# Weight loads on the hardware queue and a rearranged prologue, in a Fourier transform with a maxout layer

## The chip, the cores and the metric

The kernel runs on one core of a Trainium2 chip. The metric is the device time of one execution in microseconds (us), as the median of several runs. Engine names are those of the profile: PE multiplies matrices, DVE is the vector engine, ACT the scalar engine, POOL is GpSimd, SP starts transfers. POOL starts transfers too, on the software queue (q0 in the profile). SP's transfers go through the hardware queue (q1).

## The reference

```python
x: (8, 3072, 256) float32
X = fft(x, axis=1);  X = fft(X, axis=2);  y = X.real        # 2-D Fourier transform, real part
y = y.reshape(24576, 256)
h = maximum(maximum(y @ w1, y @ w2), y @ w3)                # w1, w2, w3: 256 x 768
out = h @ w_out                                             # w_out: 768 x 256
```

## The kernel before

Each of the 8 batches is one Fourier transform of 3072 rows. It is split as 24 × 128: stage `s` (`Mix.s`, L474 and L476) multiplies the rows of x by small 24-point tables, with the rows in forward order (`nat` for batch 0, `x0` after that) and in reversed order (`back`, the second half of `x0`). ACT or DVE evict the result to `z` (L481). Stage `k` (`Mix.k`, L500 and L502) multiplies `z` by the tables `tab`, and ACT evicts to `t` (L504). The tables have 13 rows of three parts each: a sine, a shifted sine, and the first part negated (`tab_minus`, L272).

The transform over the 256 columns is linear, so it is folded into the weights. With its table `md`, `prep_first` makes from `d2 = w2 - w1` and `d3 = w3 - w1` the folded weights `gE` (even part), `gO` (odd part) and `gD` (`gO` times a column `dif`). Half `jh` 0 or 1 of the 768 hidden columns is done at a time, four PE banks each: `gE` is evicted by DVE (L419), `gO` by ACT, and `gD` by DVE from `gO` (L422). `prep_second` folds `w1` and `w_out` together: `g1t` (L433, three evictions), then `gw` (L442, L447), then `twice` (L451).

Each batch has 18 units: 3 blocks of 512 frequencies by 6 groups `jc` of 128 hidden columns. In a unit PE makes the sums for one half of the spectrum (`unit_plus`, L520 and L521), ACT writes their ReLU to `stmp` (L534), DVE takes the maximum with the second sum (L535, to `hp`); then PE adds `gD` (`unit_minus`, L528) and ACT and DVE do the same for the mirrored half, to `hm`. The second layer is spread over later units: `l2_even` and `l2_odd` (L558, L569), `l2_hidden` (L545); DVE makes `other` (L572) and `ot` (L595), POOL makes `even` (L575) and scatters the mirrored rows with an indirect transfer (L598).

Each engine's program is in the order in which the kernel is written out (`manual_schedule`); an engine that waits holds up all that is behind it. What is done between units is set by a hand-written table, `at(batch, unit, function)`: at a unit's end the functions entered for it write their instructions.

Before the first unit there is a prologue. POOL loads x of batch 0 in 16 transfers that also convert to bfloat16, in four groups of rows (0 to 31, 32 to 63, 64 to 95, 96 to 111; rows 112 to 127 come by other queues into `xs_a`). Then it loads the weights in halves, `w1`, `w2`, `w3` of half 0 and then of half 1 (L204). DVE and ACT meanwhile compute the tables and copy x into `nat` (`lay_rows`, L345) and `back` (`turn_rows`, L133). PE multiplies tables (35 `warm` matmuls, L691) until x is laid out. SP loads the four chunks of batch 1 (`load_chunk`, L102) behind the weights of half 0 (`first_half`). POOL converts and turns chunks 0 to 2 (`turn_chunk`, L148 and L151); chunk 3 is split between ACT (L159) and POOL (L161) in `turn_last`. `differences` (L174) is done by DVE for half 0 and by POOL for half 1. `store_rows` computes the row numbers for the scattered stores (`rows_m`).

Of the kernel before, what the change touches and what calls it, by code (L numbers as in the profile page):

```python
# [9 lines left out]
FP32 = mybir.dt.float32  # L10
# [23 lines left out]
def kernel(  # L34
# [51 lines left out]
    half_pi = consts.tile([128, 64], FP32, tag="half_pi")  # L86
    w_late = consts.tile([128, 3 * 128], FP32, tag="w_late")
    twice = consts.tile([128, 256], FP32, tag="twice")
# [9 lines left out]
    def load_rows(engs, dst, b, r0, r1, after=None):  # L98
        xr = x_rows(b)
        for g in range(4):  # L100
            eng = engs[g] if isinstance(engs, tuple) else engs
            ld = eng.dma_start(out=dst[g * 24:(g + 1) * 24], in_=xr[g, :, r0:r1, :])  # L102
            if after is not None:
                tc.add_manual_dep(ld.ins, after.ins.name, AFTER, reason="weights first")

    def load_next(eng, dst, b, after=None):
# [18 lines left out]
    raw = {}  # L125
# [43 lines left out]
    def cols(t, jh):  # L169
        return t.rearrange("p (fc j) -> p fc j", fc=2)[:, :, jh * 384:(jh + 1) * 384]  # L170
# [26 lines left out]
    for r0 in (0, 32, 64):  # L197
        load_rows(nc.gpsimd, x0v[:, r0:r0 + 32, :], 0, r0, r0 + 32)
    load_rows(nc.gpsimd, x0v[:, 96:112, :], 0, 96, 112)

    first_half = None
    for jh in range(2):
        for wsrc, wdst in zip((moe_w1, moe_w2, moe_w3), (w1_bf, *raw_w)):
            wld = nc.gpsimd.dma_start(  # L204
                out=cols(wdst, jh),
                in_=wsrc.rearrange("(fc p) j -> p fc j", fc=2)[:, :, jh * 384:(jh + 1) * 384])
        if jh == 0:
            first_half = wld
    rows_f = gen.tile([128, 12 * B], FP32, tag="rows_f")
# [14 lines left out]
    for (name, value) in (("rnd", ROUND), ("n24", -24.0)):  # L224
# [18 lines left out]
                                   op0=ALU.add, op1=ALU.subtract)  # L243
    w = gen.tile([128, 10 * 128], FP32, tag="w")
    turn = 2.0 * math.pi

    def rows_of(r0, r1):
        return (w_late if r0 >= 10 else w)[:, (r0 % 10) * 128:(r0 % 10 + r1 - r0) * 128]

# [73 lines left out]
    for (m, c, own) in ((m0f, 0, 1), (m0r, 24, 3)):  # L323
        for (o0, o1, src, by) in ((0, 24, t24[:, 48 + c:72 + c], amp[:, 0:1]),
                                  (24, 26, t24[:, c:c + 13:12], amp[:, 1:2]),
                                  (26, 50, t24[:, c:c + 24], ind24[:, own:own + 1])):
            nc.scalar.activation(out=m[:, o0:o1], in_=src, func=AX.Copy, scale=by)

    tab_minus(0, 7)
    nc.vector.tensor_scalar(out=sgn, in0=pidx, scalar1=0.0, scalar2=None, op0=ALU.is_equal)  # L330
    nc.vector.tensor_scalar(out=sgn, in0=sgn, scalar1=2.0, scalar2=-1.0,
                            op0=ALU.mult, op1=ALU.add)
    nc.vector.tensor_scalar(out=dif, in0=sgn, scalar1=1.0, scalar2=None, op0=ALU.subtract)

# [9 lines left out]
    def lay_rows(copy, xs, r0, n, d0=0, d1=33):  # L344
        copy(out=xn0[:, d0:d1, r0:r0 + n],  # L345
             in_=bass.AP(xs.tensor, xs.offset + d0, [xs.ap[0], [1, d1 - d0], [64, n]]))

    def bf_rows(r0, n):
# [7 lines left out]
    tab_angles(7, 10)  # L356
    tab_angles(10, 13)
    lay_rows(on_act, bf_rows(0, 32), 0, 32)
# [3 lines left out]
    dvec = gen.tile([128, 128], FP32, tag="dvec")  # L362
    nc.vector.scalar_tensor_tensor(
        out=dvec.rearrange("p (dl g) -> p dl g", g=4),
        in0=j128[:, 0:4].unsqueeze(1).to_broadcast([128, 32, 4]), scalar=64.0,
        in1=j128[:, 0:32].unsqueeze(2).to_broadcast([128, 32, 4]), op0=ALU.mult, op1=ALU.add)
    nc.vector.tensor_scalar(out=dvec[:, 2:4], in0=j128[:, 0:2], scalar1=64.0, scalar2=32.0,
                            op0=ALU.mult, op1=ALU.add)
    vm = gen.tile([128, 256], FP32, tag="vm")
    qm = gen.tile([128, 256], FP32, tag="qm")  # L370
    nc.vector.tensor_scalar(out=vm[:, 0:128], in0=dvec, scalar1=pidx, scalar2=64.0,
                            op0=ALU.mult, op1=ALU.add)
    nc.vector.tensor_scalar(out=vm[:, 128:256], in0=dvec, scalar1=pidx, scalar2=None,
                            op0=ALU.mult)
    nc.vector.tensor_scalar(out=vm[:, 128:129], in0=pidx, scalar1=128.0, scalar2=64.0,
                            op0=ALU.mult, op1=ALU.add)
    turn_rows(on_act, 63, 32, 54, 65)
    turn_rows(on_dve, 63, 32, 32, 54)
    lay_rows(on_dve, bf_rows(64, 32), 64, 32)
    tab_sines(7, 10, (2,))  # L380
    tab_sines(10, 13, (0,))
    for (copy, a, b, c, d) in ((on_dve, 32, 54, 0, 20), (on_act, 54, 64, 20, 33)):
        turn_rows(copy, 95, 17, a, b)
        if copy is on_act:
            turn_rows(copy, 95, 16, 64, 65)
        lay_rows(copy, bf_rows(96, 16), 96, 16, c, d)
    nc.vector.tensor_scalar(out=qm, in0=vm, scalar1=256.0 * ROUND, scalar2=None, op0=ALU.add)
    nc.vector.scalar_tensor_tensor(out=vm, in0=qm, scalar=-256.0 * ROUND, in1=vm,
                                   op0=ALU.add, op1=ALU.subtract)

    for ch in range(4):
        raw[1, ch] = load_chunk(1, ch, first_half)
    tab_minus(7, 10, nc.gpsimd)
    nc.gpsimd.memset(two_row, 0.0)
# [5 lines left out]
    nc.gpsimd.dma_start(out=wout_bf.rearrange("p (jc c) -> p jc c", jc=NJC),  # L400
# [5 lines left out]
    def prep_first(jh, bank):  # L406

        cs = slice(jh * 384, (jh + 1) * 384)
        for i, wv in enumerate((d2_bf, d3_bf)):
            for half in range(2):  # L410
                psg = bank()
                hs = slice(half * 128, (half + 1) * 128)
                for fc in range(2):
                    nc.tensor.matmul(
                        psg[:, 0:384], md[fc][:, hs],
                        wv[:, fc * DFF + jh * 384: fc * DFF + jh * 384 + 384],
                        start=(fc == 0), stop=(fc == 1))
                if half == 0:
                    nc.vector.tensor_copy(out=gE[i][:, cs], in_=psg[:, 0:384])  # L419
                else:  # L420
                    nc.scalar.copy(out=gO[i][:, cs], in_=psg[:, 0:384])
                    nc.vector.tensor_scalar(out=gD[i][:, cs], in0=gO[i][:, cs], scalar1=dif,  # L422
                                            scalar2=None, op0=ALU.mult)
                yield

    def prep_second():

        for jp in range(NJC // 2):
            pst = ps_f.tile([128, 512], FP32, name="pst", tag="ps")
            for k in range(2):  # L430
                jc = jp * 2 + k
                for fc in range(2):
# [18 lines left out]
        nc.tensor.matmul(pst[:, 0:256], two_row, gw[:, 256:512], start=True, stop=True)  # L451
        nc.vector.tensor_copy(out=twice, in_=pst[:, 0:256])
        nc.vector.tensor_scalar(out=twice[:, 0:1], in0=twice[:, 0:1], scalar1=-1.0, scalar2=None,
                                op0=ALU.add)
# [234 lines left out]
    warm = ps_s.tile([128, 512], FP32, name="warm", tag="ps")  # L689
    for _ in range(35):  # L690
        nc.tensor.matmul(warm, tab[:, 0:128], tab[:, 0:512], start=True, stop=True)  # L691
    m = Mix(0)
    x0f = (lambda d: xn0[:, d, 0:128], rows_back(xr0))
    for k in range(7):
        m.s(k, x0f, pool=ps_s if k % 4 else ps_f,
            evict=nc.vector.tensor_copy if k in (1, 3) else nc.scalar.copy)
        if k == 1:
            differences(nc.vector, 0, (0,))
        if k == 2:
            nc.scalar.activation(out=md[0], in_=vm, func=AX.Sin, scale=float(-2.0 * math.pi / 256.0))  # L700
        if k == 3:
            halves = [t.rearrange("p (q two g) -> p two q g", two=2, g=4) for t in md]
            nc.vector.tensor_copy(out=halves[1][:, 0], in_=halves[0][:, 0])
            nc.vector.tensor_scalar(out=halves[1][:, 1], in0=halves[0][:, 1], scalar1=-1.0,
                                    scalar2=None, op0=ALU.mult)
            differences(nc.vector, 0, (1,))
    slots = [ps_s, ps_s, ps_f, ps_f]
# [58 lines left out]

    def late_tables():
        tab_sines(10, 13, (1, 2))
        tab_minus(10, 13, nc.gpsimd)

    for (u, fn) in ((0, prep_some), (0, prep_some), (1, prep_some), (1, prep_some),
                    (2, lambda: m.k(2)), (2, late_tables), (2, prep_some), (2, prep_some),
                    (3, lambda: m.k(3)), (3, prep_some), (4, prep_some),
                    (5, prep_some), (5, l2_first),
                    (6, lambda: m.k(4)), (7, lambda: m.k(5)), (7, m.end),
                    (0, lambda: turn_chunk(1, 0)), (2, lambda: turn_chunk(1, 1)),
                    (5, lambda: turn_chunk(1, 2)),
                    (8, lambda: turn_last(0)), (9, lambda: turn_last(1))):
        at(0, u, fn)
# [92 lines left out]
```

## Time and profile before

| what | value |
|---|---|
| median of 3 runs | 417.44 us (417.38 to 417.55) |
| the profiled execution | 417.16 us, its span 415.3 us |
| granted PE clock, mean | 0.999 |
| PE busy | 397.7 us, 96% |
| DVE, ACT, POOL busy | 313.1, 266.8, 320.4 us |
| chain that ended last | PE 88%, POOL 4%, DVE 4% |
| first real matmul (L474) | 19.29 us |
| first `gE`/`gO` matmul of a unit (L520) | 24.95 us |
| PE at stage `s0` of batch 1 | arrives 53.19 us, goes on 54.49 us |

The span runs from the first to the last instruction; 1.86 us of the profiled execution lie outside it. A timeline row has start, duration, engine, line, operation, tiles, shape and count; in brackets is the engine's idle time before it and what ended that. A row of waits reads: who waited, for what, total us, times, longest.

### The profile page before, as it was taken

The page shows a single profiled execution, that of the slowest core. Times are in us where ns is not written, and L with a number is a line of the kernel's source. Part 1 is how long each engine was busy: PE and PEld are TensorE (multiplying, and loading weights), DVE is VectorE, ACT ScalarE, POOL GpSimd, SP SyncE. Part 2 cuts the span into 40 slices and gives each one's busy share as a digit, 9 for nine tenths or more (in the row PEclk, how much of TensorE's full clock was granted, in tenths as well). Part 3 has the DMA queues.
Part 4 walks back from the last instruction along what each step waited for, and adds up shares of the span by engine and source line. Part 5 has one row for each costly group of instructions (what it writes and reads, how often), then busy time and mean ns, then how long its engine had stood idle before and what let it go on. Part 6 is the DMA issues. An engine that isn't in the chain of part 4 may idle for free.

```text
span 415.3 us, 9110 instructions
## 1 busy us (share of the span) xinstructions
PE 397.7 (96%) x3076; PEld 269.0 (65%) x3076; DVE 313.1 (75%) x561; ACT 266.8 (64%) x488; POOL 320.4 (77%) x431
## 2 busy tenths in 40 slices
PE   1889989999999999999999999999999999999996
PEld 0455667666676677667666666666676667766665
DVE  8998766776777777687668767687678777778883
ACT  7777767666766666666775666666676666655550
POOL 9977867999988888888878788888878844445651
PEclk9999999999999999999999999999999999999999
DMA  9998895684327841396316852288312222111314
GB/s 112 165 202 176 177 230 123 153 198 109 113 76 181 199 140 65 102 218 162 104 64 165 202 112 106 88 207 179 121 52 76 66 67 76 66 65 47 108 64 140
DMA packets 130535, 52.70 MB, mean 127 GB/s; under 512 B 113073, under 2 KB 127224, under 8 KB 130488
## 3 DMA queue, kind: packets, MB, share of 16 engines
q1 hardware_dynamic: 105408, 35.93, 35.7%
q0 software_dynamic: 24144, 15.86, 16.7%
q8 instruction: 24, 0.39, 0.5%
q10 hardware_dynamic: 936, 0.33, 0.3%
q14 instruction: 23, 0.19, 0.2%
HBM read 29.02 MB, written 25.17 MB: 130 GB/s over the span
## 4 chain that ended last, share of the span: by engine, by line
PE 88%; POOL 4%; DVE 4%; issue 2%; DMA 1%; ACT 1%; POOLq 0%; DVEq 0%; ACTq 0%
PE po L545 29%; PE pse L520 14%; PE pse L528 14%; PE pse L521 14%; PE ps L476 2%; PE ps L502 2%; PE ps L474 2%; PE ps L500 2%; PE po L569 2%; PE pl L558 2%; POOL x L102 2%; DMA x<-in_x_dram 1%; DVE gD L422 1%; DMA out_dram<-ot 1%; DVE back L133 1%
## 5 line engine op out<-in xcount | busy, mean ns | idle before, releaser
L534 ACT ACTIVATE stmp<-pse 128x512 bf16<-128x512 f32 x288 | 171.3, 600 | 42.5 <-PE pse L521 29.6
L535 DVE TENSOR_TENSOR hp<-pse,stmp 128x512 bf16<-128x512 f32 x144 | 99.5, 691 | 89.0 <-ACT stmp L534 60.7
L598 POOL DMA_INDIRECT out_dram<-ot,rows_m x92 | 102.6, 1115 | 53.6 <-DVE ot L595 41.6
L520 PE MATMUL pse<-t,gE 128*128 128x512 bf16 x288 | 109.2, 379 | 2.0 <-DVE hm L535 0.7
L521 PE MATMUL pse<-t,gO 128*128 128x512 bf16 x288 | 109.0, 378 | 0.0
L535 DVE TENSOR_TENSOR hm<-pse,stmp 128x512 bf16<-128x512 f32 x144 | 99.1, 688 | 3.6 <-ACT stmp L534 3.5
L575 POOL TENSOR_TENSOR even<-even,other 128x256 f32<-128x256 f32 x92 | 66.4, 722 | 26.4 <-DVE other L572 23.3
L545 PE MATMUL po<-wout_bf,hp 128*128 128x256 bf16 x576 | 85.9, 272 | 0.0
L528 PE MATMUL pse<-t,gD 128*128 128x512 bf16 x288 | 85.6, 379 | 0.0
L545 PE MATMUL po<-wout_bf,hm 128*128 128x256 bf16 x570 | 85.3, 273 | 0.0
L545 PEld LDWEIGHTS <-hp 128*128 128x128 bf16 x576 | 56.3, 98 | 17.6 <-issue 2.4
L545 PEld LDWEIGHTS <-hm 128*128 128x128 bf16 x576 | 56.4, 98 | 16.5
L595 DVE TENSOR_TENSOR ot<-po,even 128x512 f32<-128x512 f32 x92 | 62.8, 683 | 0.3 <-POOL even L575 0.3
L148 POOL CAST x<-xs 96x544 bf16<-96x544 f32 (+2 forms) x51 | 58.6, 1155 | 4.0 <-DMA xs<-in_x_dram 4.0
L151 POOL CAST x<-xs 96x544 bf16<-96x544 f32 (+5 forms) x57 | 60.5, 1071 | 0.0
L504 ACT CAST t<-ps 128x512 bf16<-128x512 f32 x48 | 28.0, 586 | 36.1 <-PE ps L502 34.8
L481 ACT CAST z_all<-ps 128x480 bf16<-128x480 f32 x46 | 25.6, 559 | 37.8 <-PE ps L476 35.7
L528 PEld LDWEIGHTS <-gD 128*128 128x128 bf16 x288 | 27.9, 98 | 32.2
L572 DVE SCALAR_TENSOR_TENSOR other<-twice,po 128x256 f32<-128x256 f32 x92 | 43.8, 476 | 0.1
L521 PEld LDWEIGHTS <-gO 128*128 128x128 bf16 x288 | 28.1, 98 | 21.2 <-issue 2.9
L520 PEld LDWEIGHTS <-gE 128*128 128x128 bf16 x288 | 28.1, 98 | 20.2 <-DVE gE L419 1.0
L561 ACT COPY even<-pl 128x512 f32<-128x512 f32 x46 | 27.0, 588 | 9.7 <-PE pl L558 9.4
(166 smaller groups left out, 390.5 us busy)
## 6 DMA issues: line engine op xcount, KB each, us to landing
xs<-in_x_dram SPq DMA_DIRECT2D x84, 198.0 KB
out_dram<-ot SPq DMA_DIRECT2D x90, 128.0 KB
xs<-in_x_dram SPq DMA_DIRECT2D x28, 192.0 KB
raw_w<-in_moe_w_dram POOLq DMA_DIRECT2D x4, 384.0 KB
out_dram<-ot,rows_m POOLq DMA_INDIRECT x92
x<-in_x_dram POOLq DMA_DIRECT2D x12, 96.0 KB
out_dram<-ot SPq DMA_DIRECT2D x17, 64.0 KB
xs<-in_x_dram SPq DMA_DIRECT2D x32, 5.8 KB
```

Source lines behind the costliest of these rows:

```text
L148: nc.gpsimd.tensor_copy(v[:, d0:d1, ch * 32:ch * 32 + 32], xs[:, 0:32 * 64].rearrange("p (bb dl) -> p dl bb", dl=64)[:, d0:d1, :])
L151: reverse(lambda out, in_: nc.gpsimd.tensor_copy(out, in_), v[:, 33:66, :], xs, ch * 32, 33 if ch == 3 else 32, 32 + d0, 32 + d1)
L520: nc.tensor.matmul(pse[:, 0:n], gE[i][:, js], te, start=True, stop=False)
L521: nc.tensor.matmul(pse[:, 0:n], gO[i][:, js], to, start=False, stop=True)
L528: nc.tensor.matmul(pse, gD[i][:, js], to, start=False, stop=True, skip_group_check=True)
L534: nc.scalar.activation(out=stmp[:, 0:n], in_=pses[0][:, 0:n], func=AX.Relu)
L535: nc.vector.tensor_tensor(out=dst, in0=src3, in1=stmp[:, 0:n], op=ALU.max)
L545: nc.tensor.matmul(po, hcols(jc), wout_bf[:, jc * 256:(jc + 1) * 256], start=False, stop=(jc == NJC - 1), skip_group_check=True)
L572: nc.vector.scalar_tensor_tensor(out=other, in0=twice, scalar=po[:, 256:257], in1=po[:, 0:256], op0=ALU.mult, op1=ALU.subtract)
L575: nc.gpsimd.tensor_tensor(out=line[:, 256:512], in0=line[:, 0:256], in1=other, op=ALU.add)
L595: nc.vector.tensor_tensor(out=ot, in0=po, in1=lin, op=ALU.add)
L598: stored(nc.gpsimd.indirect_dma_start(out, bass.IndirectOffsetOnAxis(ap=rows_m[0:128 - lo, b * 12 + slot: b * 12 + slot + 1], axis=0), ot[ ...
```

## The change

- `w1` of half 0 stays on POOL behind x. `w2` and `w3` of both halves are loaded by SP; those of half 0 wait for the third group of x. `w1` of half 1 is loaded by POOL after `store_rows`. The chunks of batch 1 follow on SP without a wait of their own.
- A memset of `mark` on POOL waits for DVE's last copy of `nat`; POOL's memsets, `store_rows`, `w1` of half 1, `differences` and `w_out` stand behind it.
- In the last copies ACT and DVE have other shares. `dvec` goes ahead of `tab_minus(0, 7)`; `vm` and `qm` go ahead of the third group's copies on DVE, `sgn` and `dif` behind the last; the sine for `md` goes ahead of the third group on ACT.
- `gD` is made from PSUM. The first `g1t` and 255 columns of `twice` are evicted by ACT.
- The third part of the tables' rows 7 to 9 and the first part of rows 10 to 12 are made in units 0 and 2, the rest of rows 10 to 12 in unit 3. POOL's `tab_minus` for them goes to units 1 and 3; `k3` goes from unit 3 to unit 4; the first of the three `g1t` steps goes from unit 2 to unit 1. `turn_last` goes from units 8 and 9 to units 7 and 8.
- There are 32 warm matmuls.

```diff
-    first_half = None
+    load_w(nc.gpsimd, w1_bf, moe_w1, 0)      # load_w: the same transfer, on a given queue
     for jh in range(2):
-        for wsrc, wdst in zip((moe_w1, moe_w2, moe_w3), (w1_bf, *raw_w)):
-            wld = nc.gpsimd.dma_start(...)
-        if jh == 0:
-            first_half = wld
+        for wsrc, wdst in zip((moe_w2, moe_w3), raw_w):
+            ld = load_w(nc.sync, wdst, wsrc, jh)
+            if jh == 0:
+                tc.add_manual_dep(ld.ins, third.ins.name, AFTER, reason="x first")
...
+    (dvec, two instructions, from below)
     tab_minus(0, 7)
-    (sgn, dif: three instructions)
...
     tab_angles(10, 13)
+    (vm[:, 0:128], from below)
     lay_rows(on_act, bf_rows(0, 32), 0, 32)
     tab_sines(7, 10, (0, 1))
     turn_rows(on_dve, 31, 32, 32, 65)
     lay_rows(on_dve, bf_rows(32, 32), 32, 32)
-    (dvec; vm[:, 0:128])
     (vm[:, 128:256]; vm[:, 128:129])
-    turn_rows(on_act, 63, 32, 54, 65)
-    turn_rows(on_dve, 63, 32, 32, 54)
-    lay_rows(on_dve, bf_rows(64, 32), 64, 32)
-    tab_sines(7, 10, (2,))
-    tab_sines(10, 13, (0,))
-    for (copy, a, b, c, d) in ((on_dve, 32, 54, 0, 20), (on_act, 54, 64, 20, 33)):
+    (qm; vm rounded, from below)
+    nc.scalar.activation(out=md[0], in_=vm, func=AX.Sin, scale=...)
+    for (copy, a, b, c, d) in ((on_act, 54, 65, 20, 33), (on_dve, 32, 54, 0, 20)):
+        turn_rows(copy, 63, 32, a, b)
+        lay_rows(copy, bf_rows(64, 32), 64, 32, c, d)
+    for (copy, a, b, c, d) in ((on_act, 58, 64, 22, 33), (on_dve, 32, 58, 0, 22)):
         turn_rows(copy, 95, 17, a, b)
         if copy is on_act:
             turn_rows(copy, 95, 16, 64, 65)
-        lay_rows(copy, bf_rows(96, 16), 96, 16, c, d)
-    (qm; vm rounded)
+        laid = lay_rows(copy, bf_rows(96, 16), 96, 16, c, d)
+    (sgn, dif)
     for ch in range(4):
-        raw[1, ch] = load_chunk(1, ch, first_half)
-    tab_minus(7, 10, nc.gpsimd)
+        raw[1, ch] = load_chunk(1, ch)
+    first_op = nc.gpsimd.memset(mark, 0.0)
+    tc.add_manual_dep(first_op.ins, laid.ins.name, AFTER, reason="the two share a port")
     (memsets of two_row, gw)
     store_rows()
+    load_w(nc.gpsimd, w1_bf, moe_w1, 1)
     differences(nc.gpsimd, 1)
...
                     nc.scalar.copy(out=gO[i][:, cs], in_=psg[:, 0:384])
-                    nc.vector.tensor_scalar(out=gD[i][:, cs], in0=gO[i][:, cs], scalar1=dif,
+                    nc.vector.tensor_scalar(out=gD[i][:, cs], in0=psg[:, 0:384], scalar1=dif,
...
-            nc.vector.tensor_copy(out=g1t[:, jp * 512:(jp + 1) * 512], in_=pst)
+            (nc.vector.tensor_copy if jp else nc.scalar.copy)(
+                out=g1t[:, jp * 512:(jp + 1) * 512], in_=pst)
...
-        nc.vector.tensor_copy(out=twice, in_=pst[:, 0:256])
-        nc.vector.tensor_scalar(out=twice[:, 0:1], in0=twice[:, 0:1], ...)
+        nc.scalar.copy(out=twice[:, 1:256], in_=pst[:, 1:256])
+        nc.vector.tensor_scalar(out=twice[:, 0:1], in0=pst[:, 0:1], ...)
...
-    for _ in range(35):                      # warm
+    for _ in range(32):
...
         if k == 1:
-            differences(nc.vector, 0, (0,))
-        if k == 2:
-            nc.scalar.activation(out=md[0], in_=vm, func=AX.Sin, scale=...)
-        if k == 3:
             (md's other half: two copies)
+            differences(nc.vector, 0, (0,))
+        if k == 3:
             differences(nc.vector, 0, (1,))
...
-    def late_tables():
-        tab_sines(10, 13, (1, 2))
-        tab_minus(10, 13, nc.gpsimd)
-    for (u, fn) in ((0, prep_some), (0, prep_some), (1, prep_some), (1, prep_some),
-                    (2, lambda: m.k(2)), (2, late_tables), (2, prep_some), (2, prep_some),
-                    (3, lambda: m.k(3)), (3, prep_some), (4, prep_some),
-                    (5, prep_some), (5, l2_first),
+    for (u, fn) in ((0, prep_some), (0, prep_some), (0, lambda: tab_sines(7, 10, (2,))),
+                    (1, prep_some), (1, prep_some), (1, prep_some),
+                    (2, lambda: m.k(2)), (2, prep_some), (2, lambda: tab_sines(10, 13, (0,))),
+                    (3, prep_some), (3, lambda: tab_sines(10, 13, (1, 2))),
+                    (4, lambda: m.k(3)), (4, prep_some), (5, prep_some), (5, l2_first),
                     (6, lambda: m.k(4)), (7, lambda: m.k(5)), (7, m.end),
-                    (0, lambda: turn_chunk(1, 0)), (2, lambda: turn_chunk(1, 1)),
+                    (0, lambda: turn_chunk(1, 0)), (1, lambda: tab_minus(7, 10, nc.gpsimd)),
+                    (2, lambda: turn_chunk(1, 1)), (3, lambda: tab_minus(10, 13, nc.gpsimd)),
                     (5, lambda: turn_chunk(1, 2)),
-                    (8, lambda: turn_last(0)), (9, lambda: turn_last(1))):
+                    (7, lambda: turn_last(0)), (8, lambda: turn_last(1))):
```

Lines in parentheses stand for instructions that are moved or kept unchanged.

More of the change, by code (lines that the diff above doesn't have):

```diff
@@ L327 @@
             nc.scalar.activation(out=m[:, o0:o1], in_=src, func=AX.Copy, scale=by)
+    dvec = gen.tile([128, 128], FP32, tag="dvec")
+    nc.vector.scalar_tensor_tensor(
+        out=dvec.rearrange("p (dl g) -> p dl g", g=4),
+        in0=j128[:, 0:4].unsqueeze(1).to_broadcast([128, 32, 4]), scalar=64.0,
+        in1=j128[:, 0:32].unsqueeze(2).to_broadcast([128, 32, 4]), op0=ALU.mult, op1=ALU.add)
+    nc.vector.tensor_scalar(out=dvec[:, 2:4], in0=j128[:, 0:2], scalar1=64.0, scalar2=32.0,
+                            op0=ALU.mult, op1=ALU.add)
     tab_minus(0, 7)
[L330 to L333, printed above, removed]
     back = gen.tile([96, 33 * 130], BF16, tag="back")
@@ L344, in lay_rows @@
     def lay_rows(copy, xs, r0, n, d0=0, d1=33):
-        copy(out=xn0[:, d0:d1, r0:r0 + n],
-             in_=bass.AP(xs.tensor, xs.offset + d0, [xs.ap[0], [1, d1 - d0], [64, n]]))
+        return copy(
+            out=xn0[:, d0:d1, r0:r0 + n],
+            in_=bass.AP(xs.tensor, xs.offset + d0, [xs.ap[0], [1, d1 - d0], [64, n]]))
     def bf_rows(r0, n):
@@ L357 @@
     tab_angles(10, 13)
+    vm = gen.tile([128, 256], FP32, tag="vm")
+    qm = gen.tile([128, 256], FP32, tag="qm")
+    nc.vector.tensor_scalar(out=vm[:, 0:128], in0=dvec, scalar1=pidx, scalar2=64.0,
+                            op0=ALU.mult, op1=ALU.add)
     lay_rows(on_act, bf_rows(0, 32), 0, 32)
@@ L361 @@
     lay_rows(on_dve, bf_rows(32, 32), 32, 32)
[L362 to L372, printed above, removed]
     nc.vector.tensor_scalar(out=vm[:, 128:256], in0=dvec, scalar1=pidx, scalar2=None,
@@ L385 @@
             turn_rows(copy, 95, 16, 64, 65)
-        lay_rows(copy, bf_rows(96, 16), 96, 16, c, d)
-    nc.vector.tensor_scalar(out=qm, in0=vm, scalar1=256.0 * ROUND, scalar2=None, op0=ALU.add)
-    nc.vector.scalar_tensor_tensor(out=vm, in0=qm, scalar=-256.0 * ROUND, in1=vm,
-                                   op0=ALU.add, op1=ALU.subtract)
+        laid = lay_rows(copy, bf_rows(96, 16), 96, 16, c, d)
+    nc.vector.tensor_scalar(out=sgn, in0=pidx, scalar1=0.0, scalar2=None, op0=ALU.is_equal)
+    nc.vector.tensor_scalar(out=sgn, in0=sgn, scalar1=2.0, scalar2=-1.0,
+                            op0=ALU.mult, op1=ALU.add)
+    nc.vector.tensor_scalar(out=dif, in0=sgn, scalar1=1.0, scalar2=None, op0=ALU.subtract)
     for ch in range(4):
-        raw[1, ch] = load_chunk(1, ch, first_half)
-    tab_minus(7, 10, nc.gpsimd)
+        raw[1, ch] = load_chunk(1, ch)
+    first_op = nc.gpsimd.memset(mark, 0.0)
+    tc.add_manual_dep(first_op.ins, laid.ins.name, AFTER, reason="the two share a port")
     nc.gpsimd.memset(two_row, 0.0)
@@ L451, in prep_second @@
         nc.tensor.matmul(pst[:, 0:256], two_row, gw[:, 256:512], start=True, stop=True)
-        nc.vector.tensor_copy(out=twice, in_=pst[:, 0:256])
-        nc.vector.tensor_scalar(out=twice[:, 0:1], in0=twice[:, 0:1], scalar1=-1.0, scalar2=None,
+        nc.scalar.copy(out=twice[:, 1:256], in_=pst[:, 1:256])
+        nc.vector.tensor_scalar(out=twice[:, 0:1], in0=pst[:, 0:1], scalar1=-1.0, scalar2=None,
                                 op0=ALU.add)
```

21 lines of the change are left out of this document (13 added, 8 removed).

## The prediction

> **What bounds the kernel now.** I read the page first: TensorE (PE) is busy for 96% of the span and carries 88% of the chain that ended last.
>
> ```profile
> PE 397.7 (96%) x3076; PEld 269.0 (65%) x3076; DVE 313.1 (75%) x561; ACT 266.8 (64%) x488; POOL 320.4 (77%) x431
> ...
> PE 88%; POOL 4%; DVE 4%; issue 2%; DMA 1%; ACT 1%; POOLq 0%; DVEq 0%; ACTq 0%
> ```
>
> Then the waits of PE. Cut to the first 56 us, the view gives all that the whole run has but 0.5 us: 0.24 at 75.09 on `t` and 0.26 at 92.15 on `ot`, both made from PE's own results shortly before, so they move along with PE.
>
> ```profile
> PE warm L691 <- DVE sgn L330: 8.9, 1, 8.9
> PE ps L474 <- DVE nat L345: 1.2, 1, 1.2
> PE ps L476 <- POOL x L161: 1.1, 1, 1.1
> PE pse L520 <- DVE hm L535: 0.7, 2, 0.4
> PE pse L520 <- DVE gE L419: 0.5, 1, 0.5
> ...
> PE psg L414 <- DVE md_all L704: 0.3, 1, 0.3
> ```
>
> So from some 55 us on PE runs practically without a wait, and no edit touches that part. The change is worth exactly the shift of PE's arrival there. I take the first matmul behind stage `s0` of batch 1 as the finish line: L520 at 54.88. The timeline of PE gives the stations before it.
>
> ```profile
> 19.29 0.20 PE L474 MATMUL ps<-m24f,nat 96*128 96x96 bf16 x1 [1.23 <-DVE nat L345]
> ...
> 26.54 0.81 PE L414 MATMUL psg<-d_bf,md_all 128*128 128x384 bf16 x4
> ...
> 53.19 0.21 PE L474 MATMUL ps<-m24f,x 96*128 96x96 bf16 x1
> 54.49 0.22 PE L476 MATMUL ps<-m24r,x 96*128 96x96 bf16 x1 [1.09 <-POOL x L161]
> ```
>
> The second station needs `d2` of weight half 1, which POOL makes from `w1` and `w2`; here PE does not wait for it. Last I read POOL's timeline, then DVE's and ACT's.
>
> ```profile
> 14.85 0.76 POOL L204 DMA_DIRECT2D w_bf<-in_moe_w_dram  x1
> ...
> 17.02 1.26 POOL L204 DMA_DIRECT2D w_bf<-in_moe_w_dram  x1
> ...
> 20.89 0.22 POOL L394 MEMSET two_row<- 128x128 bf16 x1
> ...
> 22.84 0.79 POOL L220 CAST rows_m<-rows_f 128x96 int32<-128x96 f32 x1
> 23.82 1.64 POOL L174 TENSOR_TENSOR d_bf<-raw_w,w_bf 128x768 bf16<-128x768 f32 x1 [0.19 <-DMA raw_w<-in_moe_w_dram]
> ...
> 27.42 0.93 POOL L400 DMA_DIRECT2D wout_bf<-in_moe_w_out_dram  x1
> ```
>
> ```profile
> 16.76 1.41 DVE L345 COPY nat<-x 96x1056 bf16<-96x1056 bf16 x1
> ...
> 23.43 0.54 DVE L419 CAST gE<-psg 128x384 bf16<-128x384 f32 x1
> 23.91 1.66 DVE L422 TENSOR_SCALAR gD<-gO,dif 128x384 bf16<-128x384 bf16 x1
> ...
> 28.58 0.31 DVE L422 TENSOR_SCALAR gD<-gO,dif 128x384 bf16<-128x384 bf16 x1
> ```
>
> ```profile
> 47.95 1.14 ACT L159 CAST x<-xs 96x544 bf16<-96x544 f32 x1
> ```
>
> The same `gD` costs 0.31 alone and 1.66 while POOL runs L174 (23.82 to 25.46): the two engines shut each other out when both work from SBUF.
>
> **The change, part by part.** *Start of PE's real work.* DVE's last copy of `nat` ended at 19.15. Third and fourth copies there took 0.90 + 1.41 + 0.62 + 0.51 = 3.44 us beside POOL's issues; the 1056-element copy took 1.07 at 13.57, so a quiet one saves about 0.3, and cutting columns off DVE's share (`nat` 33 to 20 columns in the third, more `back` in the fourth) saves a further 0.4 on DVE, with ACT's share fitting because two sines (0.61 and about 0.5) leave it. `dvec` and `vm` go ahead of copies that wait for data; `qm` and its partner (0.69) also move ahead, so they eat part. I put the end of DVE's copies at 18.4 (18.1 to 18.9) and PE's start at 18.45, 0.85 earlier. The three fewer warm matmuls (0.65 us) and `dvec`'s delay of the warm start by about 0.4 lie inside PE's idle 1.23: nothing; without that cover they would cost their size.
>
> *PE up to `d2` of half 1.* 26.54 less 0.85, less the stall on `md_all` (0.34; its sine now stands ahead of the third copies), less the one on `gE` (0.55; `gD` ahead of it costs 0.54, `gE`'s row from the same PSUM shape, in place of 1.66): PE could be there at 24.8. `w2` and `w3` of half 0 are read by DVE at about 20.3 and landed at 19.30 and 20.62 before, with `w1` of half 1 behind them; SP issues them from 15.3, behind the third quarter of x. The same bytes in the same order: nothing.
>
> *The new wait.* `w1` of half 1 was issued at 17.02. Now it stands on POOL behind the `mark` that waits for DVE's last copy (18.4), and behind memsets, iotas and `rows_m`: 20.89 to 23.63, 2.74 us. Queued behind it on POOL are `d2`, `d3`, `wout` and all of batch 1's turning; PE waits for `d2`. The issue costs 0.76 (bounds 0.76 and 1.26, the two rows of `w1`; I take the first, since no tail of x is issued then). From the end of the issue to landing, no row has this situation. `w1` of half 0: 15.60 to 18.35, 2.75. `wout`, twice the bytes, issued while SP's chunks were moving: 28.35 to 32.90, 4.55. Two halves of weights landed 1.0 apart, which with 0.75 of start gives 1.75 as a floor. I take 2.75, same size and queue, and keep 1.75 and 4.55. Then `d2`, 1.64, and 0.15 for hand-overs: 18.4 + 2.74 + 0.76 + 2.75 + 1.64 + 0.15 = 26.44 against 26.54. The whole lead of 1.7 is eaten: -0.1.
>
> The Trainium skill speaks here ("DMA: Bandwidth & Descriptors", Queues, rings and completion order): a DMA engine takes turns, packet by packet, between the queues that have work. By it `w1` would share with SP's chunks, its 1.2 us of transfer would double, and the sum below would end 1.2 higher, near 417.9. The trace disagrees: from 30.5 to 32.0 the software queue (`wout`) moved 150 to 167 GB/s while the hardware queue, with chunks issued, got 1 to 28.
>
> The same skill ("SBUF — State Buffer", the trap of DVE blocking DMA) says that a DVE operation holding the shared port keeps GpSimd from writing descriptors. That would make 1.26 the price of the issue, 0.5 more; the two rows of `w1` (0.76 and 1.26, the second beside DVE's copies) agree in direction.
>
> *From there to `l2`.* DVE is relieved of `gD` (four rows, 1.66 + 1.63 + 0.31 + 1.24 = 4.84, to 4 × 0.54 = 2.16), of one `g1t` (0.68) and of `twice` (0.42). Little of that is on the path: PE's stalls at 30.13 (0.41, on a `stmp`) and 32.27 (0.24, on ACT's `t`). I count 0.45 of these 0.65, since ACT takes over `g1t` (about 0.6) and `twice` (about 0.45) and two late sines: -0.45. `tab_minus` of rows 7 to 10 now stands behind the turning of chunk 0: 33.6 + 1.2 gives 34.8, and `k3`, moved from 34.00 to unit 4, comes at about 35.2. `wout` lands near 33.8; it is read from 35.7. Both margins are under 2 us and shrink with each us that `w1` is late; if POOL is a further 0.5 late, `k3` waits.
>
> *Units 7 to 9.* ACT's two copies of the last chunk (1.14 and 1.09) go one unit earlier, so the first now stands behind `t` (0.59) and `t_mid` (0.17), ahead of unit 7's two ReLUs, which before started at 46.81. They end some 1.06 later; DVE's `hp`, `hm` and the L595 that frees `po` queue behind, and PE has almost no slack there: +1.05 (bounds 0 and 1.14).
>
> *Start of batch 1.* POOL's reversals (1.16 and 1.19) follow ACT's chunk and one `even` fewer stands before the last: done by 52.9 at the latest. The wait of 1.09 goes; from L474 at 53.19 to L476 at 54.49 it is 1.30, against 0.05 unhindered: -1.25. Next to be late is nothing that I can see; PE arrives at 53.7.
>
> **Sum.** -0.1 - 0.45 + 1.05 - 1.25 = -0.75. The profiled execution took 417.16 (span 415.3, 1.86 around it), so 416.41; it was 0.28 under the median of the runs, 417.44, so 416.7 on the median's scale. 0.83 us (0.2%) is about what a measurement can tell here.
>
> **Rivals.**
> *Cheaper.* `w1` lands in 1.75 rather than 2.75 (-1.0), or ACT's copy finds slack in unit 7 (-1.05). For: halves of weights did land 1.0 apart at 300 to 400 GB/s. Against: `w1` of half 0 needed 2.75, and ACT had no gap over 0.32 between 44.0 and 51.5. Either gives 415.7.
> *Slower: `w1` behind the traffic.* SP is now free to start chunks at about 19 to 20, so the queues are full when `w1` is issued. If it needs `wout`'s 4.55, `d2` is ready at 28.24, 1.7 later than PE was there before; with -0.45 + 1.05 - 1.25 the run ends 1.05 later and `k3` waits up to 0.5 more: 418.2 to 418.8, say 418.5. It decides from the point where `w1` takes over 4.3 us (the sum passes +0.83). For: `wout`'s row is the only one beside SP's chunks. Against: it has twice the bytes, and the software queue went ahead of the other. The turn-taking rule above, with 3.95, would end below that point.
> *The silence doesn't shorten the copies.* If the hardware weight loads delay x's last rows (landed 16.78), DVE ends at 19.2 as before; `mark` and everything on POOL is 0.8 later: 417.5.
>
> **How the numbers follow.** Forecast 0.46, by itself 416.0 to 417.2, spread half and half over the bound of 416.61 (0.22 faster, 0.24 same). Cheaper 0.25, faster. Slower 0.19 (0.18 slower, 0.01 same). No shorter copies 0.10 (0.07 same, 0.03 slower). Faster 0.47, same 0.32, slower 0.21. The range reaches from below the cheaper case, 415.4, to 418.4, just short of the worst; both cheap ends at once (414.7) and the worst are left out.
>
> **What would show it.** Right: the first L474 near 18.45 without more than 1 us of idle; `gD` at 0.54 in all four rows; a new PE wait at L414 on POOL L174 of 1 to 2 us, starting near 24.8 and ending near 26.4; a wait of about 1 us near units 8 and 9 that leads back to ACT L159; no wait at L476. Wrong: PE waiting at L414 past 27.5, or at `k3` for POOL's L272 (slower); no wait at L414, or none near unit 9 (cheaper); any wait of PE after 56 us that was not there before.

## The result and the profile after

The changed kernel took 420.12 us (median of 6, 419.66 to 421.79) against 417.50 for the kernel before on the same chip: a ratio of 1.0067, 95% interval 1.0049 to 1.0085. In a second comparison on another chip it was 1.0114 (1.0092 to 1.0136). The forecast was 416.7 with a range up to 418.4. Every ratio below is against the kernel before, run in the same group and on the same chip; it is formed from all runs of the two, so it need not equal the quotient of two medians.

The page of the changed kernel, engines, the PE clock by slices, and the chain:

```profile
PE 401.0 (96%) x3073; PEld 271.8 (65%) x3073; DVE 309.2 (74%) x559; ACT 267.8 (64%) x491; POOL 318.1 (76%) x428
...
PEclk9969999999999999999999999999999999999999
...
PE 84%; POOL 8%; DMA 2%; issue 2%; DVE 2%; ACT 1%; SPq 0%; POOLq 0%; DVEq 0%; ACTq 0%
```

POOL has doubled its share of the chain and DMA its own, and a slice near 25 us has a 6 where PE's clock was full before. The waits of PE:

```profile
...
PE ps L482 <- DVE sgn L392: 2.1, 1, 2.1
PE pse L528 <- ACT stmp L542: 0.8, 2, 0.5
PE pse L528 <- DVE hm L543: 0.5, 2, 0.2
...
```

There are fewer waits than before, and the wait at `s0` of batch 1 is gone. Nor is there a wait for `d2` of half 1: the new wait that the prediction gave as a sign of being right did not show in this profile. What was lost is in PE's timeline, at the stations of the prediction (line 482 is the old 474, 421 the old 414):

```profile
20.78 0.24 PE L482 MATMUL ps<-m24f,nat 96*128 96x96 bf16 x1 [2.09 <-DVE sgn L392]
...
25.86 1.48 PE L421 MATMUL psg<-d_bf,md_all 128*128 128x384 bf16 x4
...
29.95 0.81 PE L421 MATMUL psg<-d_bf,md_all 128*128 128x384 bf16 x4
```

PE begins 1.49 later than before. Stage `s` takes 5.08 us (20.78 to 25.86) where it took 2.74, and the four matmuls at 25.86 took 1.48 instead of 0.81. The busy time by windows says why: PE is busy throughout, at half clock. In such a row the number behind the five engines, 0.50, is the granted clock; the last two are DMA share and GB/s.

```profile
21.00:24.00 3.00, 3.00 (x41) 3.00 (x39) 1.50 (x5) 1.12 (x2) 2.29 (x9) 0.50 1.05 271
24.00:27.00 3.00, 3.00 (x32) 2.47 (x31) 2.08 (x4) 1.41 (x4) 0.00 (x0) 0.50 0.91 143
```

What held the start up stands in DVE's timeline, and beside it POOL's and SP's:

```profile
19.74 0.53 DVE L134 COPY back<-x 96x442 bf16<-96x442 bf16 x1 [2.82 <-DMA x<-in_x_dram]
```

```profile
15.37 1.06 POOL L203 DMA_DIRECT2D w_bf<-in_moe_w_dram  x1
20.70 0.09 POOL L398 MEMSET mark<- 1x1 f32 x1 [4.27 <-DVE sgn L392]
...
22.87 0.80 POOL L203 DMA_DIRECT2D w_bf<-in_moe_w_dram  x1
27.05 3.25 POOL L175 TENSOR_TENSOR d_bf<-raw_w,w_bf 128x768 bf16<-128x768 f32 x2 [3.39 <-DMA w_bf<-in_moe_w_dram]
```

```profile
14.92 1.94 SPq L203 DMA_DIRECT2D raw_w<-in_moe_w_dram  x4
```

x's last rows (96 to 111) landed at 19.6 instead of 16.8. POOL finished issuing them at 15.37; SP had begun to issue `w2` at 14.92. The finish line of the prediction (the first L520, now L528, behind `s0` of batch 1) moved from 54.88 to 57.64, +2.76; the span moved from 415.3 to 418.3.

`w1` of half 1 was late as well: POOL could start `d2` only at 27.05 and had it ready at 28.7. PE came for it at 29.95, so in this profile the later start and the half clock hid that lateness. But the half clock is not what makes all six runs slow: two of them, at 420.14 and 419.83, had a mean clock of 0.999 and 1.0. No trace of these two is kept.

### The profile page after: what moved, and what is told of

The parts are those of the page before. It is cut to its first block, busy times and chain, and to the rows that moved or that the text cites. A ratio compares the mean times of both kernels' runs of the same rounds, so it can differ in the third digit from the quotient of the medians.

```text
span 418.3 us, 9109 instructions
## 1 busy us (share of the span) xinstructions
PE 401.0 (96%) x3073; PEld 271.8 (65%) x3073; DVE 309.2 (74%) x559; ACT 267.8 (64%) x491; POOL 318.1 (76%) x428
## 4 chain that ended last, share of the span: by engine, by line
PE 84%; POOL 8%; DMA 2%; issue 2%; DVE 2%; ACT 1%; SPq 0%; POOLq 0%; DVEq 0%; ACTq 0%
PE po L553 27%; PE pse L528 14%; PE pse L536 13%; PE pse L529 13%; POOL x L102 3%; PE ps L482 3%; PE ps L484 3%; PE po L577 2%; PE ps L510 2%; PE pl L566 2%; PE ps L508 2%; POOL x L152 1%; POOL x L149 1%; DMA x<-in_x_dram 1%; DMA xs<-in_x_dram 1%
## 5 line engine op out<-in xcount | busy, mean ns | idle before, releaser
L542 ACT ACTIVATE stmp<-pse 128x512 bf16<-128x512 f32 x288 | 171.1, 600 | 42.9 <-PE pse L529 30.8
L528 PE MATMUL pse<-t,gE 128*128 128x512 bf16 x288 | 109.2, 379 | 1.9 <-ACT stmp L542 0.8
L583 POOL TENSOR_TENSOR even<-even,other 128x256 f32<-128x256 f32 x92 | 66.4, 722 | 25.5 <-DVE other L580 23.4
L529 PEld LDWEIGHTS <-gO 128*128 128x128 bf16 x288 | 28.1, 98 | 22.5 <-issue 4.5
L528 PEld LDWEIGHTS <-gE 128*128 128x128 bf16 x288 | 28.1, 98 | 19.3 <-issue 0.7
```

What stands on the lines that cost most here:

```text
L528: nc.tensor.matmul(pse[:, 0:n], gE[i][:, js], te, start=True, stop=False)
L529: nc.tensor.matmul(pse[:, 0:n], gO[i][:, js], to, start=False, stop=True)
L542: nc.scalar.activation(out=stmp[:, 0:n], in_=pses[0][:, 0:n], func=AX.Relu)
L583: nc.gpsimd.tensor_tensor(out=line[:, 256:512], in0=line[:, 0:256], in1=other, op=ALU.add)
```

## The experiments

**First group.** Theory A: x's last rows are late, all else follows. Theory B: `w1` of half 1 is late.

`w2` and `w3` behind the fourth group of x:

```diff
-    load_rows(nc.gpsimd, x0v[:, 96:112, :], 0, 96, 112)
+    third = load_rows(nc.gpsimd, x0v[:, 96:112, :], 0, 96, 112)
```

> One word of the changed kernel altered: w2 and w3 on the hardware queue wait for the fourth group of x rows instead of the third. Theory A (the hardware weight loads slow x's last rows: they landed at 19.6 instead of 16.8, so PE started at 20.8 and then ran at half clock): x's last rows land by 17, PE starts by 18.8 at full clock, and the time falls by 2.5 to 4 us, to 416 to 417.6. Theory B (the late w1 of half 1, issued behind the mark, sets the time): w1 still lands 3 to 4 us after its issue, PE waits for d2 of half 1 instead, and the time stays at 419 or above.

Measured: 421.08, ratio 1.0089 (1.0064 to 1.0115). The time is that of theory B. Theory A was half right: x's last rows landed at 17.1 and PE began at 18.70. But then the other load was late:

```profile
20.71 0.80 POOL L203 DMA_DIRECT2D w_bf<-in_moe_w_dram  x1
28.53 3.23 POOL L175 TENSOR_TENSOR d_bf<-raw_w,w_bf 128x768 bf16<-128x768 f32 x2 [7.02 <-DMA w_bf<-in_moe_w_dram]
```

From the end of its issue `w1` of half 1 took 6.9 us, not the 3 to 4 of theory B, and PE waited 4.0 for `d2`. The view of the transfers from 21.5, where the issue ended, to 23.5 has one queue alone, the hardware queue:

```profile
q1 hardware_dynamic: 535, 0.69, 99.5%
```

All weights back on POOL, in the order of before (`load_w(nc.gpsimd, ...)` for `w1`, `w2`, `w3` of each half; the chunks behind half 0):

> The changed kernel with all weight loads back on POOL in the old order (w1, w2, w3 of half 0, then of half 1) and SP's chunks behind half 0 as before; mark, copies, gD from PSUM, tables and units stay changed. Theory A: x's last rows land by 17, PE starts at 18.6 to 19.2 at full clock and does not wait for d2 of half 1 (its weights landed at 21.6 and 22.7 in the kernel before): 415 to 416.7, faster than before. Theory C (the other edits, ACT's copies in units 7 and 8 above all, cost by themselves): 417.5 to 418.5.

Measured: 417.85, ratio 1.0029 (1.0011 to 1.0047). PE began at 18.47, but waited 1.15 and 0.51 for `d2` and `d3` of half 1, whose weights landed at 24.3 and 27.0, and 0.91 at `k3` for POOL's `tab_minus`. This is in the range of theory C and outside that of theory A. So the weights' queue and order are more than half of the loss (1.0067 and 1.0114 with them), and a part stays.

The kernel before with `w2` and `w3` on SP alone:

```diff
-            wld = nc.gpsimd.dma_start(
+            wld = (nc.gpsimd if wdst is w1_bf else nc.sync).dma_start(
...
+            if jh == 0 and wdst is not w1_bf:
+                tc.add_manual_dep(wld.ins, third.ins.name, AFTER, reason="x first")
```

> The kernel before with one edit alone: w2 and w3 issued by SP behind the third group of x, nothing else. Theory A: x's last rows land at about 19.6, PE's first real matmul at about 20.7 behind an idle of 2.6 us or more and at half clock for some us: 418.5 to 421. Theory B: w1 is loaded early on POOL, so there is nothing to wait for: 416.5 to 417.8.

Measured: 416.62, ratio 0.9987 (0.9975 to 0.9998), twelve runs from 415.9 to 417.3. Theory A failed here: x's last rows landed at 16.8. In these runs the hardware queue as such cost nothing; `w1` of both halves is issued early in them. That this is not enough by itself is shown further on by the both-edits kernel of the second group and by the last kernel of the third.

41 warm matmuls in the changed kernel:

> The changed kernel with 41 warm matmuls instead of 32, so that PE has work until about 20.7. If the half clock after PE's idle of 2.1 us costs time: stage s takes 2.75 us instead of 5.1, PE comes to d2 of half 1 at about 27.6 and there waits for POOL (28.7), so of 2.3 us some 1.0 to 1.3 is left: 418.9 to 419.2 against 420.1. If the clock is the same with and without the idle, or PE's waits for POOL take all of it: 419.9 to 420.3.

Measured: 421.51, ratio 1.0104 (1.0087 to 1.012): no gain, and neither expectation met. Its profiled execution was its fastest, 418.1; there x landed at 17.1 although the kernel waits for the third group as the changed one does, and PE waited 0.55 for `d2`. The other six runs were at 421.1 to 422.4 with a clock of 0.995 or 0.996. As the profile is not one of these, it doesn't tell what held them.

**Second group**, with the changed kernel again.

> The changed kernel once more, beside the next three. Ratio to the kernel before 1.005 to 1.009. Theory D (beside the hardware weight loads any software load is late, now x's last rows, now w1 of half 0 or 1, and which one it is changes from run to run): PE comes to d2 of half 1 at 28.5 to 31, whether its first real matmul is at 18.7 or at 21. Theory A (x's last rows alone): the first real matmul is again at 20.5 or later.

Measured: 421.91, ratio 1.0114, more than expected. In its profile `d2` came when theory D expected it: this time PE began on time, and `w1` was late.

```profile
18.57 0.21 PE L482 MATMUL ps<-m24f,nat 96*128 96x96 bf16 x1
...
30.90 1.44 PE L421 MATMUL psg<-d_bf,md_all 128*128 128x384 bf16 x4 [5.79 <-POOL d_bf L175]
```

```profile
20.37 0.80 POOL L203 DMA_DIRECT2D w_bf<-in_moe_w_dram  x1
29.21 3.23 POOL L175 TENSOR_TENSOR d_bf<-raw_w,w_bf 128x768 bf16<-128x768 f32 x2 [8.05 <-DMA w_bf<-in_moe_w_dram]
```

The view of the transfers from 19.5 to 22.5 shows what the engines did: `w1` of half 0 ended in the first of these 3 us, `w1` of half 1 was issued from 20.4 on, and all but 0.01 MB was hardware traffic.

```profile
q1 hardware_dynamic: 857, 1.11, 102.6%
q0 software_dynamic: 17, 0.01, 2.1%
```

`w1` of half 1 right behind `w1` of half 0:

```diff
-    load_w(nc.gpsimd, w1_bf, moe_w1, 0)
+    for jh in range(2):
+        load_w(nc.gpsimd, w1_bf, moe_w1, jh)
...
     store_rows()
-    load_w(nc.gpsimd, w1_bf, moe_w1, 1)
```

> The changed kernel with w1 of half 1 issued on POOL right behind w1 of half 0, ahead of the mark; w2 and w3 still on the hardware queue behind the third group of x. Theory B (the late issue of w1 of half 1 is the cost): POOL's d2 of half 1 starts by 24, PE does not wait for it, 416 to 417.5. Theory A (x's last rows are): PE still starts at 20.5 or later in most runs, 419 to 420.5. Theory D: better than the changed kernel by 1 to 3 us, and uneven from run to run.

Measured: 417.23, ratio 1.0012 (0.9993 to 1.0031), beside 421.91 for the changed kernel on the same chip. This one move returns 4.7 us. In its profile x's last rows were late again (landed 19.3), yet PE did not wait for `d2`, and the finish line is at 54.59. So late x, at full clock, was made up for by what the other edits gain.

```profile
PE ps L482 <- DVE sgn L393: 1.4, 1, 1.4
```

```profile
26.87 0.81 PE L421 MATMUL psg<-d_bf,md_all 128*128 128x384 bf16 x4
```

Nine of its runs are at 416.3 to 417.6 with a mean clock of 0.999 or more; three are at 418.6 to 420.5 with 0.992 to 0.996.

Both edits:

> Both: w2 and w3 wait for the fourth group of x, and w1 of half 1 is issued right behind w1 of half 0. Theories A, B and D agree that no software load is then late for long: PE starts at 18.4 to 18.8, POOL's d2 of half 1 starts at 23.5 to 25 and PE waits for it 0 to 1 us; with the 0.65 gained behind that point 415.8 to 417.3, level with the kernel before. If the other edits of the prologue cost by themselves (theory C), 418 or more.

Measured: 419.52, ratio 1.0046 (1.0028 to 1.0063). The time is in the range of theory C, but no theory had the cause. Now `w1` of both halves is ahead and landed at 18.8 and 21.7, and `w2` of half 0, issued at 17.1, only at 23.2: DVE waited 2.99 for it, PE 3.02 for DVE, and the clock fell to half again.

```profile
24.31 1.46 PE L421 MATMUL psg<-d_bf,md_all 128*128 128x384 bf16 x4 [3.02 <-DVE d_bf L175]
```

The chunks of batch 1 behind `w1` of half 1, on top of the first experiment (`load_chunk(1, ch, w1_late)`):

> The kernel of the first experiment (w2 and w3 behind the fourth group of x; w1 of half 1 late) with SP's chunks of batch 1 also made to wait until w1 of half 1 has landed. If it was the chunks that held w1 up from 24 on: w1 lands at 24.5 to 25.5 instead of 28.4, PE waits for d2 some 0.5 to 1.5 us instead of 4.0, and the time falls by 2 to 3.5 us, to 417.5 to 419. If it was w2 and w3 alone: w1 lands at 25.5 or later still, and the time stays within 1 us of the first experiment's 421, or rises, as the chunks come later.

Measured: 419.15, ratio 1.0046 (1.0031 to 1.0061), some 1.8 us less than the first experiment by the two ratios. With no chunk moving until it was in, `w1` landed at 27.3, 5.9 us after its issue, against 6.9 with the chunks. The landing is the one expected from `w2` and `w3` alone; the time lies between the two expectations. Nor do `w2` and `w3` explain all of it: the last of them had landed at 25.5, and for the 1.8 us from there no hardware packet moved, only the last 31 packets of `w1`. What held these is open.

```profile
29.03 0.81 PE L421 MATMUL psg<-d_bf,md_all 128*128 128x384 bf16 x4 [2.65 <-POOL d_bf L175]
```

**Third group.** `w2` and `w3` of half 1 behind `w1` of half 1 (`load_w23(1, load_w(nc.gpsimd, w1_bf, moe_w1, 1))`, the chunks behind them):

> The changed kernel with w2 and w3 of half 1 (still on the hardware queue) made to wait until w1 of half 1 has landed, and the chunks behind them on SP. Theory E (an engine serves the queues' transfers about in the order in which they came: w1 of half 1 stood behind 1.5 MB of w2 and w3 that were queued first): with only half 0 ahead w1 lands 2 to 3 us after its issue, at 23 to 24.5, w2 of half 1 2 us behind, POOL's d2 starts at 25.5 to 27 instead of 29.2, and the time falls to 417.3 to 419 (chunk 0 comes later, so k3 may wait 1 us). Theory F (a software load is slow beside hardware traffic of any order, or has a fixed time of 5 us or more): w1 lands at 26 or later, w2 after 28, POOL's d2 starts after 28.5: 421.5 or more.

Measured: 424.14, ratio 1.0174 (1.015 to 1.0197). For theory E the time was a miss, as x was late (start at 20.69) and the two loads now stand in series. `w1`, `w2` and `d2` came as late on the clock as theory F says; from its issue `w1` took no longer than theory E says. The transfers from 23.6 to 26.5, with nothing else moving:

```profile
q0 software_dynamic: 272, 0.20, 52.0%
```

`w1` landed at 26.50, 2.93 after the end of its issue (23.57). That rules out a fixed time of 5 us. It doesn't decide between the two theories beyond that, as `w2` and `w3` of half 0 had landed by 20.3 and nothing moved beside `w1`.

The early `w1` with 41 warm matmuls:

> The changed kernel with w1 of half 1 early (as in the second group of runs, 416.3 to 417.6 with some runs at 418.6 to 420.5 and a mean clock of 0.992 to 0.996) and 41 warm matmuls instead of 32. If the uneven slow runs there come from PE's idle before its first real matmul and the half clock behind it: no run above 418.3, clock 0.998 or more in all, median 416.3 to 417.3. If they come from late loads alone: the same two groups of runs.

Measured: 417.17, ratio 1.0004 (0.9991 to 1.0016). All twelve runs lie between 415.9 and 418.2 with a clock of 0.999 or 1.0, though x landed at 20.6 and PE began at 21.76 in the profiled one. All three expectations were met. It fits that the uneven runs of the early `w1` came from the half clock behind PE's idle time; three of twelve runs against none of twelve, on two chips, is not more than that.

`gD` from PSUM alone, in the kernel before:

> The kernel before with gD made from PSUM, nothing else. The port is no longer fought over: gD takes 0.54 to 0.62 in all four rows instead of 1.66, 1.63, 0.31 and 1.24; the PE stalls at 26.1 (0.55) and 30.1 (0.41) shrink or go. But the s0 wait of 1.1 on POOL's reversal stands behind it and its end depends on POOL and ACT: the gain shows only as far as POOL comes earlier too. 416.6 to 417.3, within 0.2% of before.

Measured: 416.75 against 417.04, ratio 1.0007 (0.9988 to 1.0026), no difference, as expected. All four `gD` took 0.61 or 0.62 and the stalls at 26.1 and 30.1 are gone. In the profile the finish line is 0.86 earlier (54.02) with the `s0` wait still 1.09.

That kernel's edits with `w2`, `w3` on SP, `g1t`, `twice` and `turn_last` as changed:

> The kernel before with w2 and w3 on the hardware queue (w1 of both halves early on POOL), gD from PSUM, the first g1t and twice on ACT, and turn_last in units 7 and 8; prologue copies, tables and k3 as before. From the runs so far: stage up to d2 of half 1 as in the third experiment (28.2 at d3), behind it 25.8 instead of 26.4: finish line at 54.0 against 54.9, 415.8 to 416.4, faster than before by 0.15 to 0.3%. If turn_last in units 7 and 8 costs what it saves when the tables are not moved: 416.6 to 417.2.

Measured: 417.16, ratio 1.0019 (0.9994 to 1.0043); no gain. Six of twelve runs are at 416.1 to 416.7, of which three are in the expected range, the rest up to 421.3. In the profiled one, at 420.72, x's last rows landed at 20.1 and PE idled 2.83. Up to `d2` this kernel differs from the one with `w2` and `w3` on SP alone only in `gD`, and that one had no run above 417.3; why x was late here is open.

**Fourth group.** The edits behind `d2` alone, all weights on POOL as before (`gD`, `g1t`, `twice`, `turn_last` in units 7 and 8):

> The kernel before, all weights on POOL as there, with gD from PSUM, the first g1t and twice on ACT, and turn_last in units 7 and 8. By the profiles so far: with gD alone d3 of half 1 stood at 27.9 (28.5 before); behind it 25.8 instead of 26.4, since the s0 wait of 1.1 goes and 0.6 to 0.85 at unit 9 comes. Finish line at 53.7 to 54.0 against 54.9: 415.8 to 416.4, faster than before by 0.15 to 0.3%. If the terms of the prediction behind d2 were right only by chance (the changed kernel was late there, which gave POOL and ACT time): no gain, 416.7 to 417.3.

Measured: 417.79, ratio 1.0008 (0.9989 to 1.0028), no gain. The `s0` wait is gone, but unit 9 gives it back:

```profile
48.98 0.38 PE L521 MATMUL pse<-t,gE 128*128 128x512 bf16 x1 [1.30 <-ACT stmp L535]
```

ACT waited 0.82 there for chunk 3 of batch 1, with unit 7's ReLUs behind it.

The changed kernel with weights on POOL and `tab_minus` of rows 7 to 9 ahead of `store_rows`:

> The changed kernel with all weights on POOL in the old order, and POOL's tab_minus of rows 7 to 9 behind the memsets again, ahead of store_rows, instead of in unit 1. The mark, the copies, gD from PSUM and the units stay. The PE wait of 0.9 at k3 goes; the waits for d2 and d3 of half 1 (1.15 and 0.5) stay, as they hang on the landing of w2 and w3. 416.3 to 417.2 (417.9 with tab_minus late). If the mark and the other copies cost more than that: 417.5 or more.

Measured: 418.43, ratio 1.0014 (0.9997 to 1.0032). The wait at `k3` is gone as expected. The time is in the upper range, that of a cost of the mark and the copies, but the kernel before was at 417.31 on that chip, the interval of the ratio contains 1, and the two kernels with weights on POOL overlap in their intervals. What the mark costs by itself is too small for these runs. The profiled execution was the slowest of the twelve, 421.26: there the last piece of `w2` of half 1 landed at 27.0, when 15 of 16 had landed by 24.2, and PE waited for `d2`. So a load can be late with all weights on POOL too.

```profile
28.87 1.44 PE L421 MATMUL psg<-d_bf,md_all 128*128 128x384 bf16 x4 [3.47 <-POOL d_bf L175]
```

**Who is late: the order of issue.** The eight profiled executions in which `w2` waits for the third group of x split by one thing, whether POOL had finished issuing x when SP began with `w2`:

| kernel | x's issue over, POOL goes on to `w1` | first `w2` issue | last x landed |
|---|---|---|---|
| `w2`, `w3` on SP in before | 14.86 | 15.12 | 16.8 |
| changed, again | 14.98 | 15.24 | 16.9 |
| changed, 41 warm | 15.22 | 15.47 | 17.1 |
| changed | 15.37 | 14.92 | 19.6 |
| `w1` early | 15.37 | 15.04 | 19.3 |
| `w1` early, 41 warm | 15.35 | 14.98 | 20.6 |
| half 1 behind `w1` | 15.41 | 15.18 | 19.5 |
| before with `w2`, `w3` on SP and the later edits | 15.35 | 14.92 | 20.1 |

The three kernels that wait for the fourth group had it at 17.1 to 17.3. In the changed kernel x's last rows and `w2` moved side by side: both queues had packets, and from 18.0 to 18.5 their packets' times added up to 82% (x) and 70% (`w2`) of the 16 DMA engines' time. The view from 16 to 19:

```profile
q1 hardware_dynamic: 416, 0.61, 78.6%
q0 software_dynamic: 575, 0.06, 31.1%
```

Why POOL is done at 14.9 in one execution and at 15.4 in another is open; the kernel before showed 14.85.

## Why the prediction was wrong

**The step that failed** is "From the end of the issue to landing": 2.75 was taken for `w1` of half 1, 4.55 as the upper end. It measured 3.3 in the changed kernel's first profile, 6.9 with x on time in the first experiment, 8.0 in the second profile. Alone it takes 2.93, so 2.75 was about the price of an empty queue and the wrong one here. That this step matters most is shown by the early `w1`: with that load moved and nothing else, 4.7 us came back.

The rows were misread too. Counted to the last of its 16 pieces, `w1` of half 0 landed at 18.69 in the kernel before, 3.09 after its issue, not at 18.35; and `wout` at 34.95, 6.6 after its issue, not at 32.90. The upper end should have been 6.6, and the slower rival, by the prediction's own sum, 2 us worse. `d2` was ready at 28.7 (27.05 and half of 3.25) and 30.8, not at 26.44. In the first profile only 0.55 of this came from the landing; 2.30 came through `mark`, which ran at 20.70 and not at 18.4, as x was late; what stands between it and the issue took 2.17 instead of 2.74.

The bound failed because the row of `wout` was read the wrong way. As the software queue moved 150 to 167 GB/s and the hardware queue 1 to 28 there, the prediction concluded that software loads go ahead. For `w1` of half 1 the order of queueing fits better: 1.5 MB of `w2` and `w3` were queued ahead of it, and from 21.5 to 23.5 of the first experiment no packet of it moved, while the chunk that was queued behind `wout` in the kernel before landed beside or after it. That order is the rule is not shown: x's last rows and `w2` moved side by side.

The Trainium skill's rule that a DMA engine takes turns between queues ("DMA: Bandwidth & Descriptors", Queues, rings and completion order) was nearer in its sign: it spoke against this move. Its size is not what the stretches with `w1` show: the software queue had nothing for 2 us of the first experiment (0 of 0.69 MB). Elsewhere both queues moved at once, as in the view of x and `w2` above.

**The second step that failed** is "The same bytes in the same order: nothing". With `w2` on another queue the order against x was no longer fixed. The third rival had the mechanism ("the hardware weight loads delay x's last rows") at 0.8 us; x came 2.8 later. Once it did, the mark, DVE and PE moved with it.

**Not in the sum at all** was PE's clock. Three warm matmuls fewer were costed at nothing under an idle of 1.23. With x late the idle was 2.09, and stage `s` took 2.34 longer at half clock. Without the half clock PE would have met `d2`, ready at 28.7, so at most 1.25 of the arrival at 29.95 would have been saved. The first profile adds up so: +1.49 (start) + 2.34 (clock in stage `s`) - 0.42 (from there to `d2`: the stalls on `md_all` and `gE`, 0.89, gone, the rest of the half clock added) = +3.41, which is the 29.95 against 26.54. In the second profile the start was -0.72 (forecast -0.85), and the wait of 5.79 made it +4.36.

The Trainium skill says that the clock falls back when PE was idle for a free-running window of about 3.4 us ("TensorE: Matmul & The Clock Gate", Part 1: The HAM clock gate). Here it fell after idles of 2.0 (half 1 behind `w1`), 2.1 (changed) and 2.8 (the last kernel of the third group) and stayed full after 1.4 (early `w1`) and 2.65 (chunks behind `w1`, where the four matmuls behind it took 0.81). So the length of the idle alone doesn't decide; that fits a window which doesn't start with the idle, and gives no safe length near 2 us.

**Behind `d2`** the forecast was -0.65 (-0.45 + 1.05 - 1.25). In the first profile, `d3` stood at +3.42 (31.90 against 28.48) and the finish line at +2.76, so -0.66. The sum agrees, the terms do so only in part. The `s0` wait went for 1.26. Units 7 to 9 cost 0.85, of which 0.60 are the two waits at 52.01 and 52.85. The relief of DVE gave 0.23, half of what was forecast. That the total met is in part luck, for it doesn't hold whatever stands ahead: in the first kernel of the fourth group the two waits at unit 9 came to 1.55, and the stretch was 0.5 longer than before (27.70 to 54.61 against 28.48 to 54.88), as ACT came to chunk 3 before it had landed. The early `w1`, with `d3` only 0.34 later than before, kept -0.64; there SP began the chunks at 17.05 instead of 21.78, and ACT did not wait. The prediction moved ACT's copies a unit earlier and priced the work queued behind them, but not the landing of what they read.

`gD` from PSUM took 0.61 instead of the 0.54 taken from `gE`'s row, and no longer met POOL: right, and worth nothing that these runs can measure.

## What to carry to other kernels

A load that is issued late behind bulk traffic, even on another queue, can cost far more than alone (here 6.9 and 8.0 us against 2.93); issue the small load that gates the critical path early, take its price from a row with the same traffic ahead, and read its landing to the last piece. Then look at what it pushes back, as `w2` of half 0 with both edits. When a load moves to another queue, write down which transfers were ordered by the old queue alone, and order them again. Two loads released within half a microsecond of each other changed places from run to run here, so one profile doesn't show the kernel.

## What the runs showed that was not expected

With loads issued on both queues, the software queue could be at nothing for 2 us (`w1`), and the hardware queue nearly so for 1.5 us (1 to 28 GB/s in the kernel before). The last of a load's 16 pieces can lag: with the chunks held back, 13 pieces of `w1` had landed by 25.6 and the last came at 27.3, with no other load issued behind it. And a late start at full clock was made up for: with `w1` early PE began 1.2 us late (20.50), came to `d2` of half 1 at 26.87 against 26.54, as the stalls of 0.89 on the way were gone, and to the finish line 0.3 earlier than before.
